# A reordered start, and model-axis results in frequency order with a new planner figure, in an attention-plus-Fourier kernel

## The chip, the cores and the metric

One Trainium2 chip, one core. The metric is device time of one execution in microseconds (us). TensorE is called PE below (its weight loads PEld), VectorE is DVE, ScalarE is ACT, GpSimd is POOL.

Words used below: to turn is to transpose on TensorE. TensorE is warm where it runs at full rate and cold where it runs at half rate, as with four score matmuls that take 0.92 us in one place and 1.65 us in another; the gate is the clock gate that the prediction cites. A line of a trace is start and duration in us, engine, line of the kernel, operation, output<-inputs and count; in brackets stands how long the engine was idle before and what ended that wait (the releaser). A ratio with two numbers behind it is given with its 95% interval.

## The reference, cut to what matters

```python
# q, k, v: (4 batches, 8 heads, 768, 64) fp32; sampled_blocks: (24, 3)
scores = scale * q @ k.T                         # per head
mask   = window | first/last block | sampled blocks   # 24 x 24 blocks of 32
attn   = softmax(where(mask, scores, -1e9)) @ v
x      = attn, heads side by side                # (4, 768, 512)
mixed  = real(fft(fft(x, axis=1), axis=2))       # sequence axis, then model axis
u      = x + mixed
un     = (u - mean(u)) / sqrt(var(u) + 1e-6)
out    = u + relu(un @ w_ch1) @ w_ch2            # 512 -> 2048 -> 512
```

## The kernel before

Attention runs in 96 slots of two units (a unit is one chunk of 128 keys for one half of the queries of a head pair). The Fourier and channel work of a batch is done between the attention slots of the next one. So the mixing of the first batch runs between the slots of the second; I call the last part of this, about 220 to 300 us, "the stage". The order in which an engine gets its instructions is fixed when the kernel is built: a small planner keeps a clock for each engine, and takes the next piece of mixing work when the durations it has been told say that it fits.

```python
def d(us, fn, *args):                      # a piece of VectorE work, told to last `us`
    return "d", lambda: fn(*args), 0.0, 0.0, us
...
ar = [[d(1.7 if m == 1 and half == 1 else 1.3, arrive, half, m) for m in range(T)]
      for half in range(2)]
...
def gap(rest=0.0, ahead=None, kinds="tm"):
    ...
    while apart:
        kind, fn, pe, act, dve, need = apart[0]
        ...
        if kind in "dw":
            ...
            if max(when["DVE"], state["ready"]) + dve > when["PE"] + rest + ahead:
                break
```

The start: k and q of the first head pair are turned on TensorE in the one bank of pool "t", and q's six copies go out on VectorE, behind both tables of the block mask.

```python
spread_q(off_q[0:NB, :], maskT)
twice(off_q)
spread_q(keep_q[0:NB, :], keep)            # second table, needed later
...
def turn(n, a, half):
    tp, at = ps_t.tile([P, 512], FP32, tag="t", name="tp"), bank("t")
    ...
    for c, part in enumerate(parts):
        nc.tensor.transpose(tp[:, c * P:(c + 1) * P], part, ident)
    ...
        copy = nc.vector.tensor_copy if n == 0 else nc.scalar.copy
        for to, to_jump, frm, jump, cnt, step in _TURNED[half]:
            copy(out=_grid(dst, to, 2, to_jump, cnt, 1),
                 in_=_grid(tp, frm, 2, jump, cnt, step))
```

The model axis: five products make the cosine and sine parts of one block of 128 rows, even frequencies first and odd ones after them. `arrive` then adds them to two row blocks of x, each with four additions of 127 or 128 columns and one of two.

```python
def across(m):
    across_p(ps, slice(0, P), ks)          # even cosine (two products), odd cosine
    ...
    nc.tensor.matmul(ps[:, KD:KD + QD - 1], zs[:, 0, ks], sd_sb[:, 0:QD - 1],
                     start=True, stop=True)
    nc.tensor.matmul(ps[:, KD + QD - 1:512], zs[:, 1, ks], sd_sb[:, QD - 1:KD - 2],
                     start=True, stop=True)
    ...
def arrive(half, m):
    ...
    for src, up, op in ((un[:, KD:512], half == 0, ALU.subtract),
                        (un[:, 2:KD], half == 1, ALU.add)):
        for odd in range(2):
            n = QD - 1 + odd
            at = src[:, 0:QD - 1] if odd == 0 else src[:, QD - 1:KD - 2]
            f = 1 if odd else 2
            xs = _run(x, f if up else DM - f, n, 2 if up else -2)
            tt(out=xs, in0=xs, in1=at, op=op)
```

From the second batch on GpSimd adds up the softmax terms, beside VectorE:

```python
if c == 1:
    nc.gpsimd.tensor_add(out=acc_of[n, half], in0=e_of[u - 1], in1=e)
elif c > 1:
    nc.gpsimd.tensor_add(out=acc_of[n, half], in0=acc_of[n, half], in1=e)
```

Of the kernel before, what the change touches and what calls it, by code (L numbers as in the profile page):

```python
# [11 lines left out]
FP32 = mybir.dt.float32  # L12
BF16 = mybir.dt.bfloat16
U8 = mybir.dt.uint8
I32 = mybir.dt.int32
# [72 lines left out]
def kernel(  # L88
# [165 lines left out]
    def bit(n):  # L254
# [8 lines left out]
    load_q(0)  # L263

    nc.scalar.activation(out=sm.tile([P, 1], FP32, tag="nm", name="nm"), in_=neg_half,
                         func=ACT.Exp)
    load_v(0, nc.scalar)

    nc.vector.memset(maskT, 0.0)
    for base, cm, pat, fill in (  # L270
# [17 lines left out]
    twice(of_k)  # L288
    kb_i = bit(1).bitcast(I32)
    nc.gpsimd.iota(kb_i, pattern=[[0, 1]], base=0, channel_multiplier=1)  # L290
    kb = bit(1)
# [16 lines left out]
    twice(off_q)  # L308
    spread_q(keep_q[0:NB, :], keep)

    def mask_step(i):
# [29 lines left out]
    def table_d(src, dst):  # L341
# [7 lines left out]
        def put():  # L349
            if dst is cd_sb:  # L350
                nc.vector.memset(alt, 0.0)
                for to, frm in ((dst, raw), *((alt[g:g + 1, :], row) for g in (0, 32, 64))):
                    nc.vector.tensor_copy(out=to[:, 0:1], in_=frm[:, KD - 1:KD])
                    nc.vector.tensor_copy(out=to[:, 1:QD + 1], in_=frm[:, 0:KD - 2:2])
                nc.vector.tensor_copy(out=dst[:, QD + 1:KD], in_=raw[:, 1:KD:2])
            else:
                nc.vector.tensor_copy(out=dst[:, 0:QD - 1], in_=raw[:, 2:KD - 2:2])
                nc.vector.tensor_copy(out=dst[:, QD - 1:KD - 2], in_=raw[:, 1:KD:2])
                nc.vector.tensor_copy(out=dst[0:1, QD - 1:KD - 2], in_=row[:, 1:KD:2])
# [68 lines left out]
    def turn(n, a, half):  # L428
# [4 lines left out]
        dst = turned[n, a]  # L433
        tp, at = ps_t.tile([P, 512], FP32, tag="t", name="tp"), bank("t")
        if a == 0:
# [6 lines left out]
        if a == 1:  # L442
            nc.scalar.copy(out=dst[:, half * HS:(half + 1) * HS], in_=tp[:, 0:HS])
            give(at, busy("ACT", 0.5, done))
        else:
            copy = nc.vector.tensor_copy if n == 0 else nc.scalar.copy
            for to, to_jump, frm, jump, cnt, step in _TURNED[half]:
                copy(out=_grid(dst, to, 2, to_jump, cnt, 1),
                     in_=_grid(tp, frm, 2, jump, cnt, step))
                end = busy("DVE" if n == 0 else "ACT", 0.27 if cnt > 1 else 0.18, done)  # L450
            give(at, end)
# [161 lines left out]
    def fourier(b, xA, xB, uns):  # L613
# [94 lines left out]
        def across_p(ps, rows, ks):  # L708
            zc, zl = st["zc"], st["zs"][0:96, 2, :]
            mm = nc.tensor.matmul  # L710
            mm(ps[rows, 0:QD + 1], zc[:, 0, ks], cd_sb[:, 0:QD + 1], start=True, stop=False)
            mm(ps[rows, 0:QD + 1], zl[:, ks], alt, start=False, stop=True)
            mm(ps[rows, QD + 1:KD], zc[:, 1, ks], cd_sb[:, QD + 1:KD], start=True, stop=True)

        def across(m):
# [5 lines left out]
            if m == 1:  # L721
# [3 lines left out]
                give(bank("t"), when["PE"] + 2.0)  # L725
            nc.tensor.matmul(ps[:, KD:KD + QD - 1], zs[:, 0, ks], sd_sb[:, 0:QD - 1],
                             start=True, stop=True)
            nc.tensor.matmul(ps[:, KD + QD - 1:512], zs[:, 1, ks], sd_sb[:, QD - 1:KD - 2],
                             start=True, stop=True)
# [3 lines left out]
            if m == 1:  # L733
                nc.scalar.copy(out=st["zs"][0:1, 0, 0:KD], in_=end[0:1, 0:KD])
            tt(out=un[:, KD:512], in0=ps[:, KD:512], in1=un[:, 2:KD], op=ALU.subtract)
            tt(out=un[:, 2:KD], in0=ps[:, KD:512], in1=un[:, 2:KD], op=ALU.add)  # L736

        def arrive(half, m):
# [3 lines left out]
            if m == 1 and half == 1:  # L742
                row = st["zs"][0:1, 0, :]
                nc.vector.tensor_copy(out=un[0:1, 0:KD], in_=row[:, 0:KD])
                nc.vector.tensor_scalar(out=un[0:1, KD:512], in0=row[:, 2:KD],
                                        scalar1=-1.0, scalar2=None, op0=ALU.mult)
            for src, up, op in ((un[:, KD:512], half == 0, ALU.subtract),
                                (un[:, 2:KD], half == 1, ALU.add)):
                for odd in range(2):
                    n = QD - 1 + odd  # L750
                    at = src[:, 0:QD - 1] if odd == 0 else src[:, QD - 1:KD - 2]
                    f = 1 if odd else 2
                    xs = _run(x, f if up else DM - f, n, 2 if up else -2)
                    tt(out=xs, in0=xs, in1=at, op=op)
            xs = _run(x, M, 2, -M)
            tt(out=xs, in0=un[:, 0:2], in1=xs, op=ALU.add)

# [24 lines left out]
        def d(us, fn, *args):  # L782
# [6 lines left out]
        pq = [("m", lambda m=m: across(m), 2.6 if m == 1 else 1.6, 0.7, 0.95) for m in range(T)]  # L789
        ar = [[d(1.7 if m == 1 and half == 1 else 1.3, arrive, half, m) for m in range(T)]  # L790
              for half in range(2)]
# [368 lines left out]
    turn(0, 1, 0)  # L1160
    turn(0, 0, 0)
    w_loads()
    for sl in range(B * SB + 1):
# [112 lines left out]
```

## Time and profile before

| | before |
|---|---|
| time, median (range), the first 3 of the 4 runs below | 1135.9 us (1134.07 to 1137.52) |
| profiled span | 1132.1 us |
| TensorE busy | 1079.4 us (95%) |
| first scores start | 11.10 us |
| the stage, 232.07 to 305.61 us | 73.54 us, of which TensorE busy 61.55 |

The prediction shows and reads the page, the table by windows and the two soft places. One thing it does not show is where the wait of 2.54 us before the last transposes comes from. This is VectorE of the kernel before just ahead of it:

```profile
287.71 1.39 DVE L779 TENSOR_SCALAR un<-x,st 128x512 f32<-128x512 f32 x1
...
291.75 0.55 DVE L779 TENSOR_SCALAR un<-x,st 128x512 f32<-128x512 f32 x1 [1.83 <-POOL st L769]
292.75 0.55 DVE L779 TENSOR_SCALAR un<-x,st 128x512 f32<-128x512 f32 x1 [0.46 <-POOL st L769]
```

VectorE itself is idle for 1.83 us there: the normalising row needs a reciprocal root that GpSimd makes between its sums. So the chain is TensorE for VectorE for GpSimd.

### The profile page before, as it was taken

To read this page: it belongs to the slowest core of one execution; us is meant where nothing else is said; L and a number is where in the kernel's file an instruction comes from. 1 tells how busy PE (TensorE), PEld (TensorE's weight loads), DVE (VectorE), ACT (ScalarE), POOL (GpSimd) and SP (SyncE) were. 2 spreads that over 40 slices of the span, in tenths; PEclk is the share of its full clock that TensorE was granted. 3 is DMA by queue.
4 is the path that set the end of the run, shared out by engine and by line. 5 is a ranking of instruction groups with operands and counts; after the bars stand their busy time and mean duration, and the time that the engine had idled before them with its cause. 6 is when DMAs were issued, how large, how long until landed. Compare 5 with 4: busy or idle time off the path is not lost.

```text
span 1132.1 us, 11978 instructions
## 1 busy us (share of the span) xinstructions
PE 1079.4 (95%) x4284; PEld 516.3 (46%) x4284; DVE 643.9 (57%) x1195; ACT 391.4 (35%) x809; POOL 250.1 (22%) x182
## 2 busy tenths in 40 slices
PE   6999988978899999999999999999999999999997
PEld 2333333433445545444444555454354555544553
DVE  4888888488764634554459455544456355533431
ACT  4888755545212012354443211244330202210110
POOL 1000067557300000244536100243440001000000
PEclk9999999989899999999999999999999999999999
DMA  6757321011000000201111000111000001000001
GB/s 196 209 165 221 95 53 46 15 43 43 1 0 1 1 0 10 65 24 43 34 23 28 1 0 1 50 48 29 1 1 0 1 1 29 28 1 0 1 0 59
DMA packets 65184, 44.27 MB, mean 39 GB/s; under 512 B 52814, under 2 KB 57948, under 8 KB 65116
## 3 DMA queue, kind: packets, MB, share of 16 engines
q1 hardware_dynamic: 63228, 42.62, 13.4%
q10 hardware_dynamic: 1856, 0.79, 0.3%
q8 instruction: 36, 0.59, 0.2%
q14 instruction: 32, 0.26, 0.1%
q0 software_dynamic: 32, 0.01, 0.0%
HBM read 37.11 MB, written 6.29 MB: 38 GB/s over the span
## 4 chain that ended last, share of the span: by engine, by line
PE 85%; DVE 8%; ACT 2%; issue 2%; DMA 1%; SPq 1%; POOL 1%; ACTq 0%; DVEq 0%; POOLq 0%
PE y L942 29%; PE z L889 15%; PE s L470 10%; PE o L512 8%; PE yp L889 7%; PE xp L889 4%; DVE e L491 3%; PE tp L440 2%; PE zp L701 1%; PE sp L559 1%; DMA wraw<-in_moe_w_ch_dram 1%; PE xt L530 1%; PE zp L672 1%; PE s L475 1%; PE sp L573 1%
## 5 line engine op out<-in xcount | busy, mean ns | idle before, releaser
L500 POOL TENSOR_TENSOR acc<-acc,e 128x768 f32<-128x768 f32 x96 | 179.3, 1868 | 110.5 <-DVE e L491 105.8
L470 PE MATMUL s<-qT,kT 64*128 64x384 f32 x768 | 164.3, 533 | 14.7 <-DVE e L491 11.5
L945 DVE TENSOR_TENSOR x<-y,x 128x512 f32<-128x512 f32 x96 | 66.3, 691 | 195.0 <-PE y L942 194.8
L491 DVE TENSOR_TENSOR e<-s,mask 128x768 f32<-128x768 f32 x144 | 131.2, 950 | 72.9 <-ACT s L489 70.2
L942 PE MATMUL y<-w_sb,hB 128*128 128x512 f32 x384 | 170.2, 594 | 1.1 <-DVE x L945 1.0
L942 PE MATMUL y<-w_sb,hA 128*128 128x512 f32 x384 | 170.6, 593 | 0.6 <-ACT zs L703 0.6
L512 PE MATMUL o<-e,vr 128*64 128x384 f32 x768 | 145.1, 499 | 0.0
L489 ACT ACTIVATE s<-s 128x768 f32<-128x768 f32 x144 | 109.6, 795 | 70.3 <-PE s L470 69.4
L942 PEld LDWEIGHTS y<-w_sb,hB 128*128 128x128 f32 x384 | 71.5, 190 | 86.8 <-issue 81.9
L942 PEld LDWEIGHTS y<-w_sb,hA 128*128 128x128 f32 x384 | 71.2, 190 | 82.5 <-issue 79.5
L894 DVE TENSOR_TENSOR hA<-z,hA 128x384 f32<-128x384 f32 x64 | 35.7, 558 | 119.8 <-PE z L889 119.8
L498 POOL TENSOR_TENSOR acc<-e 128x768 f32<-128x768 f32 x24 | 46.3, 1928 | 246.5 <-DVE e L491 184.0
L470 PEld LDWEIGHTS s<-qT,kT 64*128 64x128 f32 x768 | 63.4, 189 | 75.8 <-DVE e L491 30.4
L889 PE MATMUL z<-unT,t 128*128 128x384 f32 x256 | 93.0, 486 | 0.0
L767 POOL TENSOR_SCALAR st<-st 128x1 f32<-128x1 f32 x24 | 6.6, 274 | 347.7 <-DVE st L766 347.3
L512 PEld LDWEIGHTS o<-e,vr 128*64 128x64 f32 x768 | 46.6, 136 | 75.6 <-issue 74.0
L898 ACT ACTIVATE hA<-hA 128x384 f32<-128x384 f32 x64 | 33.4, 522 | 119.4 <-DVE hA L894 118.9
L889 PEld LDWEIGHTS z<-unT,t 128*128 128x128 f32 x256 | 48.6, 190 | 33.9
L898 ACT ACTIVATE hB<-hB 128x384 f32<-128x384 f32 x64 | 33.5, 523 | 85.4 <-DVE hB L894 85.4
L909 ACT COPY hA<-xp 128x384 f32<-128x384 f32 x32 | 15.3, 478 | 134.4 <-PE xp L889 134.4
L889 PE MATMUL xp<-unT,w_sb 128*128 128x384 f32 x128 | 48.5, 502 | 1.5 <-ACT zs L703 1.1
L889 PE MATMUL yp<-unT,w_sb 128*128 128x384 f32 x128 | 47.4, 493 | 0.2 <-DVE un L736 0.2
(172 smaller groups left out, 1239.6 us busy)
## 6 DMA issues: line engine op xcount, KB each, us to landing
wraw<-in_moe_w_ch_dram SPq DMA_DIRECT2D x32, 512.0 KB
qr<-in_q_dram SPq DMA_DIRECT2D x90, 64.0 KB
vr<-in_v_dram SPq DMA_DIRECT2D x30, 192.0 KB
kr<-in_k_dram SPq DMA_DIRECT2D x28, 192.0 KB
out_dram<-x SPq DMA_DIRECT2D x16, 128.0 KB
out_dram<-x SPq DMA_DIRECT2D x8, 256.0 KB
out_dram<-x SPq DMA_DIRECT2D x8, 126.0 KB
out_dram<-x SPq DMA_DIRECT2D x4, 252.0 KB
```

The costliest lines, as they stand in the source:

```text
L440: nc.tensor.transpose(tp[:, c * P:(c + 1) * P], part, ident)
L470: nc.tensor.matmul(s[:, i, 0:HS], kT[D * i:D * i + D, c * P:(c + 1) * P], qT[D * i:D * i + D, half * HS:(half + 1) * HS], start=True, stop ...
L489: nc.scalar.activation(out=s[:, :, 0:HS], in_=s[:, :, 0:HS], func=ACT.Exp, scale=scale)
L491: nc.vector.tensor_tensor(out=e, in0=s[:, :, 0:HS], in1=m.broadcast_to([P, 2, HS]), op=ALU.mult)
L498: nc.gpsimd.tensor_add(out=acc_of[n, half], in0=e_of[u - 1], in1=e)
L500: nc.gpsimd.tensor_add(out=acc_of[n, half], in0=acc_of[n, half], in1=e)
L512: nc.tensor.matmul(o[D * i:D * i + D, :], vt[:, i, c, :], e[:, i, :], start=(c == 0), stop=(c == C - 1))
L889: nc.tensor.matmul(to, a[:, k, :], c[:, k, :], start=(k == 0), stop=(k == ND // 2 - 1))
L894: tt(out=to, in0=ps, in1=a, op=ALU.add)
L898: nc.scalar.activation(out=h, in_=h, func=ACT.Relu)
L942: nc.tensor.matmul(y, hs[half][:, l, m * P:(m + 1) * P], w2_sb[:, 4 * r + l, :], start=(l == 0), stop=(l == 3))
L945: nc.vector.tensor_tensor(out=x[:, m, :], in0=y, in1=x[:, m, :], op=ALU.add)
```

## The change

Intent at the start: have the first scores begin earlier and at full rate. Idle products keep TensorE at work before and after the first turns; q's first turn uses its own bank; its copies alternate between VectorE and ScalarE; the second mask table goes behind them. Intent on the model axis: the products write their results to PSUM with a stride of two, so that frequencies lie in order, and `arrive` needs one addition per part of 255 columns in place of two. The planner is told 1.0 us for an `arrive` in place of 1.3.

```diff
+    def warm(n):
+        m = ps_m.tile([P, P], FP32, tag="m", name="warm")
+        for _ in range(n):
+            nc.tensor.matmul(m, ident, ident, start=True, stop=True)
+    warm(6)
 ...
+    kb_i = bit(1).bitcast(I32)          # moved up, ahead of six selects
+    nc.gpsimd.iota(kb_i, pattern=[[0, 1]], base=0, channel_multiplier=1)
 ...
-    spread_q(keep_q[0:NB, :], keep)     # moved behind the first turns
 ...
-        tp, at = ps_t.tile([P, 512], FP32, tag="t", name="tp"), bank("t")
+        first = n == 0 and half == 0
+        tag, pool = ("m", ps_m) if first and a == 0 else ("t", ps_t)
+        tp, at = pool.tile([P, 512], FP32, tag=tag, name="tp"), bank(tag)
 ...
+                on, copy = (("DVE", nc.vector.tensor_copy) if n == 0 and (half == 1 or i % 2 == 0)
+                            else ("ACT", nc.scalar.copy))
 ...   # across_p likewise for the cosine products
-            nc.tensor.matmul(ps[:, KD:KD + QD - 1], zs[:, 0, ks], sd_sb[:, 0:QD - 1],
+            nc.tensor.matmul(_run(ps, KD + 1, QD - 1, 2), zs[:, 0, ks], sd_sb[:, 0:QD - 1],
                              start=True, stop=True)
-            nc.tensor.matmul(ps[:, KD + QD - 1:512], zs[:, 1, ks], sd_sb[:, QD - 1:KD - 2],
+            nc.tensor.matmul(_run(ps, KD, QD, 2), zs[:, 1, ks], sd_sb[:, QD - 1:KD - 2],
                              start=True, stop=True)
 ...   # arrive: two halves of each part become one
+                xs = _run(x, 1 if up else DM - 1, M - 1, 1 if up else -1)
+                tt(out=xs, in0=xs, in1=src, op=op)
 ...
-        ar = [[d(1.7 if m == 1 and half == 1 else 1.3, arrive, half, m) for m in range(T)]
+        ar = [[d(1.4 if m == 1 and half == 1 else 1.0, arrive, half, m) for m in range(T)]
 ...
     turn(0, 0, 0)
+    warm(3)
+    spread_q(keep_q[0:NB, :], keep)
     w_loads()
```

Cut: the merged copies of the cosine table, and the shifted slices that follow from the new order of the frequencies.

More of the change, by code (lines that the diff above doesn't have):

```diff
@@ L288 @@
     twice(of_k)
-    kb_i = bit(1).bitcast(I32)
-    nc.gpsimd.iota(kb_i, pattern=[[0, 1]], base=0, channel_multiplier=1)
     kb = bit(1)
@@ L352, in put @@
                 for to, frm in ((dst, raw), *((alt[g:g + 1, :], row) for g in (0, 32, 64))):
-                    nc.vector.tensor_copy(out=to[:, 0:1], in_=frm[:, KD - 1:KD])
-                    nc.vector.tensor_copy(out=to[:, 1:QD + 1], in_=frm[:, 0:KD - 2:2])
+                    nc.vector.tensor_copy(out=to[:, 0:QD + 1], in_=frm[:, 0:KD:2])
                 nc.vector.tensor_copy(out=dst[:, QD + 1:KD], in_=raw[:, 1:KD:2])
@@ L445, in turn @@
         else:
-            copy = nc.vector.tensor_copy if n == 0 else nc.scalar.copy
-            for to, to_jump, frm, jump, cnt, step in _TURNED[half]:
+            for i, (to, to_jump, frm, jump, cnt, step) in enumerate(_TURNED[half]):
+                on, copy = (("DVE", nc.vector.tensor_copy) if n == 0 and (half == 1 or i % 2 == 0)
+                            else ("ACT", nc.scalar.copy))
                 copy(out=_grid(dst, to, 2, to_jump, cnt, 1),
                      in_=_grid(tp, frm, 2, jump, cnt, step))
-                end = busy("DVE" if n == 0 else "ACT", 0.27 if cnt > 1 else 0.18, done)
+                end = busy(on, 0.27 if cnt > 1 else 0.18, done)
             give(at, end)
@@ L709, in across_p @@
             zc, zl = st["zc"], st["zs"][0:96, 2, :]
+            even, odd = _run(ps[rows, :], 0, QD + 1, 2), _run(ps[rows, :], 1, QD, 2)
             mm = nc.tensor.matmul
-            mm(ps[rows, 0:QD + 1], zc[:, 0, ks], cd_sb[:, 0:QD + 1], start=True, stop=False)
-            mm(ps[rows, 0:QD + 1], zl[:, ks], alt, start=False, stop=True)
-            mm(ps[rows, QD + 1:KD], zc[:, 1, ks], cd_sb[:, QD + 1:KD], start=True, stop=True)
+            mm(even, zc[:, 0, ks], cd_sb[:, 0:QD + 1], start=True, stop=False)
+            mm(even, zl[:, ks], alt, start=False, stop=True)
+            mm(odd, zc[:, 1, ks], cd_sb[:, QD + 1:KD], start=True, stop=True)
         def across(m):
@@ L734, in across @@
                 nc.scalar.copy(out=st["zs"][0:1, 0, 0:KD], in_=end[0:1, 0:KD])
-            tt(out=un[:, KD:512], in0=ps[:, KD:512], in1=un[:, 2:KD], op=ALU.subtract)
-            tt(out=un[:, 2:KD], in0=ps[:, KD:512], in1=un[:, 2:KD], op=ALU.add)
+            tt(out=un[:, KD:512], in0=ps[:, KD:512], in1=un[:, 1:M], op=ALU.subtract)
+            tt(out=un[:, 1:M], in0=ps[:, KD:512], in1=un[:, 1:M], op=ALU.add)
         def arrive(half, m):
@@ L744, in arrive @@
                 nc.vector.tensor_copy(out=un[0:1, 0:KD], in_=row[:, 0:KD])
-                nc.vector.tensor_scalar(out=un[0:1, KD:512], in0=row[:, 2:KD],
+                nc.vector.tensor_scalar(out=un[0:1, KD:512], in0=row[:, 1:M],
                                         scalar1=-1.0, scalar2=None, op0=ALU.mult)
             for src, up, op in ((un[:, KD:512], half == 0, ALU.subtract),
-                                (un[:, 2:KD], half == 1, ALU.add)):
-                for odd in range(2):
-                    n = QD - 1 + odd
-                    at = src[:, 0:QD - 1] if odd == 0 else src[:, QD - 1:KD - 2]
-                    f = 1 if odd else 2
-                    xs = _run(x, f if up else DM - f, n, 2 if up else -2)
-                    tt(out=xs, in0=xs, in1=at, op=op)
-            xs = _run(x, M, 2, -M)
-            tt(out=xs, in0=un[:, 0:2], in1=xs, op=ALU.add)
+                                (un[:, 1:M], half == 1, ALU.add)):
+                xs = _run(x, 1 if up else DM - 1, M - 1, 1 if up else -1)
+                tt(out=xs, in0=xs, in1=src, op=op)
+            ends = x[:, 0:M + 1:M]
+            tt(out=ends, in0=un[:, 0:M + 1:M], in1=ends, op=ALU.add)
         norms = {}
```

## The prediction

> **What bounds the kernel now.** I read the page first (busy shares and the chain that ended last), then a table of stages by window, then the timeline of each stage that TensorE does not fill, and last the forms of the lines that the change touches.
>
> ```profile
> PE 1079.4 (95%) x4284; PEld 516.3 (46%) x4284; DVE 643.9 (57%) x1195; ACT 391.4 (35%) x809; POOL 250.1 (22%) x182
> ...
> PE 85%; DVE 8%; ACT 2%; issue 2%; DMA 1%; SPq 1%; POOL 1%; ACTq 0%; DVEq 0%; POOLq 0%
> ```
>
> TensorE (PE) is busy for 1079.4 of 1132.1 us and is 85% of the chain. A change that takes no TensorE work away can earn only from the 53 us of idle time, or from stretches where TensorE runs at a lower granted clock. The stages show where both lie (columns: window, PE, PEld, DVE, ACT, POOL busy us with counts, granted clock, DMA share, GB/s):
>
> ```profile
> 0.00:10.00 10.00, 1.99 (x7) 1.22 (x7) 6.61 (x37) 1.96 (x3) 3.68 (x14) 1.00 0.74 188
> 10.00:20.00 10.00, 8.90 (x44) 3.00 (x44) 1.27 (x9) 4.32 (x7) 0.00 (x0) 1.00 0.81 236
> ...
> 265.00:300.00 35.00, 28.27 (x138) 13.48 (x137) 29.04 (x44) 15.60 (x33) 21.81 (x18) 0.90 0.14 35
> 300.00:500.00 200.00, 198.82 (x659) 103.35 (x658) 108.37 (x219) 45.83 (x97) 20.70 (x21) 1.00 0.05 14
> 500.00:750.00 250.00, 248.08 (x959) 121.77 (x958) 138.09 (x235) 82.06 (x178) 75.29 (x49) 1.00 0.10 26
> ```
>
> From 300 us on TensorE is over 99% busy at full clock: there nothing on VectorE (DVE) or ScalarE (ACT) sets the end. The two soft places are the first 20 us and the end of the second attention batch (about 220 to 295 us), where DVE is busy 29.04 of 35 us and the granted clock is 0.90.
>
> The start, in order of time (start, us, engine, instruction, idle before and its releaser):
>
> ```profile
> 5.12 0.14 DVE L292 CAST scratch<-scratch 24x1 f32<-24x1 int32 x1 [0.71 <-POOL scratch L290]
> ...
> 5.44 0.87 PE L440 MATMUL tp<-ident,kr 128*128 128x128 f32 x3 [5.44 <-DMA kr<-in_k_dram]
> ...
> 6.88 1.12 PE L440 MATMUL tp<-ident,qr 128*128 128x128 f32 x4 [0.57 <-ACT kT L443]
> ...
> 9.12 1.13 DVE L245 CAST at_q<-wide 24x128 bf16<-24x128 f32 x10
> 10.18 1.12 DVE L448 COPY qT<-tp 128x128 f32<-128x128 f32 x6
> 11.10 1.65 PE L470 MATMUL s<-qT,kT 64*128 64x384 f32 x4 [3.10 <-DVE qT L448]
> ...
> 15.51 0.92 PE L470 MATMUL s<-qT,kT 64*128 64x384 f32 x4
> ```
>
> q's turn waits 0.57 us for kT's copy, because both turns use the one bank of pool "t". The first scores wait 3.10 us for qT: VectorE is spreading the second table of the block mask until 10.25, and only then makes all six qT copies. The same four score matmuls take 1.65 us there and 0.92 us at 15.51: until about 15 us the array runs at half rate.
>
> The soft stage around 220 to 295 us, first VectorE with GpSimd (POOL) beside it, in three views (wide, GpSimd's own, narrow), then TensorE:
>
> ```profile
> 222.26 3.54 DVE L754 TENSOR_TENSOR x<-x,un 128x127 f32<-128x127 f32 x4
> ```
> ```profile
> 221.63 3.83 POOL L500 TENSOR_TENSOR acc<-acc,e 128x768 f32<-128x768 f32 x2 [2.71 <-DVE e L491]
> ```
> ```profile
> 222.26 1.32 DVE L754 TENSOR_TENSOR x<-x,un 128x127 f32<-128x127 f32 x1
> ...
> 223.71 1.90 DVE L754 TENSOR_TENSOR x<-x,un 128x127 f32<-128x127 f32 x1
> ...
> 225.53 0.28 DVE L754 TENSOR_TENSOR x<-x,un 128x128 f32<-128x128 f32 x1
> ```
> ```profile
> 289.16 0.66 PE L816 MATMUL utp<-ident,un 128*128 128x128 f32 x4 [1.63 <-DVE un L779]
> 292.35 2.18 PE L816 MATMUL utp<-ident,un 128*128 128x128 f32 x8 [2.54 <-DVE un L779]
> 294.32 2.77 PE L889 MATMUL xp<-unT,w_sb 128*128 128x384 f32 x4
> ...
> 305.61 1.45 PE L889 MATMUL xp<-unT,w_sb 128*128 128x384 f32 x4
> ```
>
> The four additions of one part of the model-axis result take 3.54 us, though three other rows of the kind are 0.28 us each: the first ends when GpSimd's first sum ends, the second when its second does, the rest run free. At the stage's end TensorE has only transposes left, waits 1.63 and 2.54 us for VectorE's normalised rows, and then does the first product in 2.77 us instead of 1.45: cold again.
>
> **What the Trainium skill says.** (1) "TensorE: Matmul & The Clock Gate", Part 1: the array starts at half rate and goes to full rate after about 3.4 us of sustained work, in a free-running window. The 1.65 against 0.92 us agrees, about 4 us after the first scores. (2) The same page, Part 4: transposes don't count as busy for that gate. This fits the turns at 5.44 and 6.88 not having warmed it, and is why the added idle products are plain ident-by-ident matmuls. (3) "SBUF — State Buffer", Who interferes with whom: a VectorE instruction with two SBUF inputs and a GpSimd one that reads SBUF block each other for whole instructions. The 1.32 and 1.90 us above agree. (4) "PSUM — Partial Sum Buffer", Specifications: lines of 8 bytes, and "any non-contiguous AP slows matmuls significantly". No matmul of the kernel before writes with a stride, so its trace says nothing; after the change all five matmuls of every model-axis result do.
>
> **The change part by part.**
>
> Start. The small iota goes ahead of six GpSimd selects, so VectorE loses its 0.71 us wait: the mask chain moves from 5.12 to about 4.45, and ends its first table at 7.86 instead of 8.53. q's turn uses a bank of "m", so it follows kr's turn at 6.3 and ends near 7.4. Of the six copies three (128, 126, 126 columns) stay on VectorE, 0.6 us as half of the 1.12 plus the larger shapes; three go to ScalarE, which has only kT's copy (6.35 to 6.83). The second table's spread (8.54 to 10.18, 1.64 us) goes behind the copies; its product is first needed by the mask steps of the fourth slot, near 37 us, so it costs nothing. qT is ready at 7.86 + 0.6 = 8.5 instead of 11.1: 2.6 us earlier.
> Six idle products start when ident is ready (2.53), each two instructions of 0.22 us warm, so about 0.43 cold: 2.6 us, ended near 5.2, before kr lands at 5.44. Three more fill 7.4 to 8.7, beside the copies. Two cold units of scores took 11.10 to about 15.0, 3.9 us; two warm ones from 15.51 take 2.2. If the gate opens in time that is another 1.7 us; because its window is free-running I count 1.2. Sum: 3.8 us (2.6 to 4.3). It lasts: from 40 to 110 us TensorE is 98% busy, so nothing slack swallows it.
>
> Model axis, work. Each part's four additions (median 285 ns, 1.14 us) become two of 255 columns, 0.42 us each as the rows of that size (L735) show: 0.3 us less, 24 parts, 7 us of VectorE. After 300 us this is hidden (18 of 24 parts). In the soft stage six parts count: 6 x 0.3 = 1.8 us at most, and less where GpSimd blocks, since two additions still meet two sums. The table copies lose four small instructions: nothing on the path.
>
> Model axis, order. The planner is told 1.0 us for a part, not 1.3. Comparing the instruction orders, TensorE's order is the same in both kernels but for the start and this stage: the second model-axis product comes two slots earlier, and the six transposes of normalised rows, four of them bunched at the end before, are spread so that one is left. That takes away most of 1.63 + 2.54 us and some of the cold product after it (1.3 us). Against it, VectorE was busy 56.3 of the 67.6 us from 226.7 to 294.3, so part of the wait only moves earlier: I count 4 us saved in all, the 1.8 included (0 to 8).
>
> Model axis, TensorE. If the stride is free, 0. If it doubles the five products, 12 results x 5 x 0.22 = 13 us, plus 4 edge sets x 3 x 0.22 = 2.6 us: some 15 us, nearly all exposed.
>
> Sum without the stride: 1135.9 - 3.8 - 4.0 = 1128.1.
>
> **The rivals.** Strided PSUM writes: the skill speaks for them. Against: in the chain of waits an fp32 score product of 384 columns takes 0.42 us and a bf16 one 0.135, so at fp32 there may be time to spare between two writes. I give a clear slowdown a chance of 0.25; then 1135.9 - 7.8 + 15 = 1143.
> A wait in place of the one removed: the stage at 220 to 295 stays bound by VectorE locked against GpSimd, now with TensorE stopped in mid-slot for the earlier transposes and products; the gain is 0 to 1 and the time 1131 to 1132. For it: 11.5 us of scores already wait on the mask multiply:
>
> ```profile
> PE s L470 <- DVE e L491: 11.5, 11, 1.9
> ```
> Data that lands too late for an earlier start: q of the second pair is issued until 11.7 us and its turn moves from 19.96 to about 16; weight chunk 1 would be wanted near 20. I think both have landed; if not, 1 to 2 us of the 3.8 are lost.
>
> **Range and chances.** Most likely 1128, pulled up by the stride to 1129. A range for 8 in 10 is 1120 to 1142: the low end is 4.3 at the start and all 8 and a little from the stage with its cold stretches; the high end is the stride at nearly full cost. 2% is 22.7 us: faster than 1113 would need more than all idle of the two places, slower than 1158 more than the doubled stride.
>
> **What would show it.** Right: the first scores near 8.5 us and their four matmuls near 0.92; additions of 255 columns, 24 x 2, near 0.42 us where GpSimd is idle; one transpose group left before the first product, and the granted clock of the stage above 0.93; rows after 300 us unchanged. The model-axis products decide the stride, by this row's successor (275 means free, above 400 means slow):
>
> ```profile
> L728 PE MATMUL pq<-sd_sb,zs x24: 274/276/422, 218.0 to 925.6; 128*128 128x128 f32 x24
> ```
> I am wrong if the first scores are still cold or wait for DMA, if the stage is as long as before, or if those rows grow.

## The result, and the profile after

| | before | after |
|---|---|---|
| time, median (range), 4 runs each | 1134.99 us (1132.92 to 1137.52) | 1122.39 us (1120.79 to 1124.91) |
| ratio, 95% interval | | 0.989 (0.9859 to 0.9921) |
| profiled span, granted clock | 1132.1, 0.990 | 1122.8, 0.993 |
| first scores | 11.10 us | 9.18 us |
| the stage | 73.54 us | 64.55 us |

A ratio here and below is the mean time of one kernel's runs over that of the kernel before in the same rounds, so it is not quite the ratio of the medians. The changed kernel is 1.1% faster: within 2%, and 6.6 us below the 1129 on record.

The page of the changed kernel, and its windows (length, busy us of PE, PEld, DVE, ACT, POOL with counts, granted clock, DMA share, GB/s):

```profile
PE 1081.5 (96%) x4302; PEld 518.5 (46%) x4302; DVE 636.3 (57%) x1140; ACT 392.4 (35%) x812; POOL 250.4 (22%) x182
...
PE 86%; DVE 8%; ACT 2%; issue 2%; POOL 1%; DMA 0%; SPq 0%; ACTq 0%; DVEq 0%; POOLq 0%
```
```profile
0.00:10.00 10.00, 6.94 (x29) 5.74 (x29) 6.63 (x32) 2.56 (x6) 3.69 (x14) 1.00 0.75 192
10.00:20.00 10.00, 9.60 (x47) 3.27 (x43) 1.07 (x10) 4.92 (x10) 0.00 (x0) 1.00 0.82 238
265.00:300.00 35.00, 30.28 (x143) 15.45 (x139) 27.72 (x41) 14.91 (x32) 20.79 (x16) 1.00 0.05 12
300.00:500.00 200.00, 198.82 (x660) 103.17 (x660) 104.88 (x202) 46.39 (x99) 23.71 (x22) 1.00 0.05 14
```

TensorE's busy time has not fallen but grown by 2.1 us: the idle products at the start add 4.4 us (2.93 and 1.49). From 300 to 500 us the row is the same as before, 198.82 us busy of 200, and from the end of the stage to the end of the span it is 826.5 us before and 826.3 after. So the gain lies before that point, and the 7.6 us less of VectorE work over the whole kernel counted only where it fell.

The windows must be cut at the same work, not at the same time. From the scores of the 44th slot to the second channel product of the first batch, before and then after:

```profile
232.07:305.61 73.54, 61.55 (x301) 29.96 (x301) 59.41 (x91) 32.09 (x67) 41.74 (x32) 0.91 0.10 24
```
```profile
231.91:296.46 64.55, 55.87 (x290) 26.17 (x286) 54.96 (x78) 32.13 (x67) 41.21 (x30) 0.97 0.12 31
```

The changed kernel enters the stage at almost the same time and leaves it 9.0 us earlier. The idle time of TensorE (length less busy time) fell from 11.99 to 8.68 us; the rest is in the busy time, where the granted clock rose from 0.91 to 0.97. The counts differ because the order does, and some products fall outside the cut. A cut a little wider, 226.80 to 305.61 before and 226.66 to 296.46 after, holds 320 matmuls in both: there 4.8 us of the gain is idle time and 4.2 us is the same products at a higher clock.

The longest single wait of the old stage stands in its middle, and the prediction does not name it (TensorE, then the two VectorE lines ahead of it, all of the kernel before):

```profile
245.43 0.66 PE L440 MATMUL tp<-ident,qr 128*128 128x128 f32 x4 [3.57 <-DVE sums L543]
...
247.83 2.82 PE L470 MATMUL s<-qT,kT 64*128 64x384 f32 x8
```
```profile
242.35 2.49 DVE L754 TENSOR_TENSOR x<-x,un 128x127 f32<-128x127 f32 x4
...
244.83 0.55 DVE L543 TENSOR_TENSOR sums<-sp,sums 128x384 f32<-128x384 f32 x1
```

A turn of q waits 3.57 us because the addition into `sums` stands in VectorE's queue behind a normalised row and four model-axis additions, and the scores after it run cold (2.82 us for eight matmuls that take 1.56 warm). This wait is 3.4 to 3.6 us in each kernel with the old order and all of GpSimd's sums, and it is in none with the new order. So the order takes away 3.57 us here and 3.7 at the end (below), and a new wait of 3.13 us comes.

The stage's end in the changed kernel, the place of the 1.63 and 2.54 us:

```profile
283.23 0.63 PE L821 MATMUL utp<-ident,un 128*128 128x128 f32 x4 [0.47 <-DVE un L784]
283.70 1.46 PE L894 MATMUL xp<-unT,w_sb 128*128 128x384 f32 x4
284.99 1.45 PE L894 MATMUL yp<-unT,w_sb 128*128 128x384 f32 x4
289.57 1.56 PE L894 MATMUL z<-t,w_sb 128*128 128x384 f32 x4 [3.13 <-DVE t L858]
```

One transposed row block is left, the wait is 0.47 us, and the first product runs at 1.46 us, warm. A new wait stands behind it: 3.13 us for VectorE, whose next additions are held up:

```profile
283.00 2.30 DVE L858 TENSOR_TENSOR t<-unT 128x512 f32<-128x512 f32 x1
285.34 2.18 DVE L858 TENSOR_TENSOR t<-unT,t 128x512 f32<-128x512 f32 x1
287.44 0.68 DVE L858 TENSOR_TENSOR unT<-unT 128x512 f32<-128x512 f32 x1
```

The same addition takes 0.68 us as soon as GpSimd's sums (three of them without a pause until 286.97) are over.

The start of the changed kernel, in order of time:

```profile
2.58 2.93 PE L269 MATMUL warm<-ident 128*128 128x128 f32 x12 [2.58 <-POOL ident masks.py:199]
...
7.27 0.66 PE L447 MATMUL tp<-ident,qr 128*128 128x128 f32 x2 [0.47 <-DMA qr<-in_q_dram]
...
8.02 0.29 DVE L456 COPY qT<-tp 128x128 f32<-128x128 f32 x1
8.34 0.27 ACT L456 COPY qT<-tp 128x128 f32<-128x128 f32 x1 [1.45 <-DVE qT L456]
8.64 0.29 DVE L456 COPY qT<-tp 128x126 f32<-128x126 f32 x1 [0.33 <-ACT qT L456]
8.96 0.16 ACT L456 COPY qT<-tp 128x2 f32<-128x2 f32 x1 [0.35 <-DVE qT L456]
9.16 0.29 DVE L456 COPY qT<-tp 128x126 f32<-128x126 f32 x1 [0.23 <-ACT qT L456]
...
9.18 1.65 PE L478 MATMUL s<-qT,kT 64*128 64x384 f32 x4
```

The copies on two engines do not run side by side: each starts when the one on the other engine is over, and names it as its releaser. The first scores begin after the fourth copy, while the last two still run (to 9.64 us). And the first scores take 1.65 us, half rate, in spite of the idle products.

The products' row by form (ns: lowest, median, highest) answers the question of the stride:

```profile
L737 PE MATMUL pq<-sd_sb,zs x24: 274/275/276, 218.0 to 916.3; 128*128 128x128 f32 x24
```

275 ns as before: writing fp32 results to PSUM with a stride of two costs nothing here. The medians of the other four products of a result, which now write with a stride too, are 274 and 275 ns, before and after.

### The profile page after: what moved, and what is told of

Its sections match the earlier page's. It is cut to its first block, busy times and chain, and to the rows that moved or that the text cites. A ratio compares the mean times of both kernels' runs of the same rounds, so it can differ in the third digit from the quotient of the medians.

```text
span 1122.8 us, 11958 instructions
## 1 busy us (share of the span) xinstructions
PE 1081.5 (96%) x4302; PEld 518.5 (46%) x4302; DVE 636.3 (57%) x1140; ACT 392.4 (35%) x812; POOL 250.4 (22%) x182
## 4 chain that ended last, share of the span: by engine, by line
PE 86%; DVE 8%; ACT 2%; issue 2%; POOL 1%; DMA 0%; SPq 0%; ACTq 0%; DVEq 0%; POOLq 0%
PE y L947 30%; PE z L894 15%; PE s L478 10%; PE o L520 9%; PE yp L894 7%; PE xp L894 4%; DVE e L499 3%; PE tp L447 2%; PE zp L709 1%; PE sp L567 1%; PE xt L538 1%; PE zp L680 1%; PE s L483 1%; DVE x L759 1%; PE sp L581 1%
## 5 line engine op out<-in xcount | busy, mean ns | idle before, releaser
L894 PE MATMUL z<-t,w_sb 128*128 128x384 f32 x128 | 46.6, 487 | 3.1 <-DVE t L858 3.1
```

The source lines that it names most:

```text
L894: nc.tensor.matmul(to, a[:, k, :], c[:, k, :], start=(k == 0), stop=(k == ND // 2 - 1))
```

## The experiments

Twelve runs in three groups; each group ran on one chip and shares its 11 runs of the kernel before (medians 1134.85, 1134.67 and 1135.09 us). The experiments have 4 to 6 runs each. Where a difference is given in us below, it is the ratio's distance from 1 times 1135. Executions of one kernel lie up to 7.4 us apart (1131.43 to 1138.84 for the kernel before in the first group), so the medians alone can't place differences under 2 us; for those I read the trace.

### 1. Which part pays: four parts alone

**The planner's figures alone.** The kernel before, with nothing but the assumed duration changed. TensorE's order in the stage is then that of the changed kernel.

```diff
-        ar = [[d(1.7 if m == 1 and half == 1 else 1.3, arrive, half, m) for m in range(T)]
+        ar = [[d(1.4 if m == 1 and half == 1 else 1.0, arrive, half, m) for m in range(T)]
```

> The kernel before with one edit: the planner is told 1.0 us for a part of the model-axis result instead of 1.3, so TensorE's order is exactly that of the changed kernel, while each part is still four strided additions and the start is the old one. Theory (the order is what pays): 6 to 9 us faster than the kernel before, the stage of 220 to 295 us shorter by as much, and only one group of transposes left before the first product. Rival (the additions pay, the order only follows): 0 to 2 us faster, or slower, because TensorE now waits in mid-slot for parts that still take 3.5 us.

Measured: 1127.77 us, ratio 0.9939 (0.9916 to 0.9962), 6.9 us less. Its stage:

```profile
234.03:299.11 65.08, 55.88 (x290) 26.14 (x286) 55.56 (x86) 32.28 (x68) 41.10 (x30) 0.97 0.12 31
```

65.08 us against 73.54: one number in the planner, with not one instruction less, gives 8.5 of the 9.0 us of the stage. The end of the stage is that of the changed kernel too:

```profile
285.88 0.63 PE L816 MATMUL utp<-ident,un 128*128 128x128 f32 x4 [0.50 <-DVE un L779]
286.34 1.46 PE L889 MATMUL xp<-unT,w_sb 128*128 128x384 f32 x4
```

**The additions alone.** Frequency order and one addition per part, with the planner still told 1.3; TensorE's order is that of the kernel before.

```diff
 # the changed kernel's across_p, across, arrive, table copies; old start; and
-        ar = [[d(1.4 if m == 1 and half == 1 else 1.0, arrive, half, m) for m in range(T)]
+        ar = [[d(1.7 if m == 1 and half == 1 else 1.3, arrive, half, m) for m in range(T)]
```

> The changed kernel's results in frequency order with one addition per part, but the planner told 1.3 us as before, so TensorE's order is exactly that of the kernel before, and with the old start. Theory (order pays): 0.5 to 2 us faster than the kernel before, six parts on the path at 0.3 us at most. Rival (work pays): 5 to 9 us faster. Strided results in PSUM: if they cost anything on TensorE, this run is slower than before; the trace of the changed kernel says they do not.

Measured: 1134.95 us, ratio 0.9993 (0.9966 to 1.0019): no difference to be seen. Stage 72.25 us, and the waits at its end stand:

```profile
290.31 0.66 PE L812 MATMUL utp<-ident,un 128*128 128x128 f32 x4 [1.63 <-DVE un L775]
293.51 2.18 PE L812 MATMUL utp<-ident,un 128*128 128x128 f32 x8 [2.54 <-DVE un L775]
295.48 2.11 PE L885 MATMUL xp<-unT,w_sb 128*128 128x384 f32 x4
```

Halving the number of additions saves 1.3 us of the stage in the old order. The VectorE time of these additions from 205 to 300 us shows why: 19.03 us before, 18.20 with fewer of them, but 13.74 with only the new order and 12.93 with both. What a part costs is decided by what GpSimd does beside it. Two additions of 255 columns, in the changed kernel, once with GpSimd idle and once with it at work:

```profile
219.69 0.75 DVE L759 TENSOR_TENSOR x<-x,un 128x255 f32<-128x255 f32 x2
...
222.26 3.41 DVE L759 TENSOR_TENSOR x<-x,un 128x255 f32<-128x255 f32 x2
```

Four small additions took 3.54 us at that place. Two additions against two GpSimd sums are still two waits for a whole sum.

**The whole model axis, old start.**

```diff
 # the changed kernel without: warm, the iota's move, keep_q's move,
 # q's bank of "m", copies on two engines
```

> The whole model-axis part of the change with its planner figures, and the old start. Theory: 9 to 10 us faster than the kernel before, which is the whole gain that the two profiled traces show from 220 us on. If the start carries a large share instead, this is only 5 to 7 us faster.

Measured: 1126.91 us, ratio 0.9924 (0.9901 to 0.9946), 8.6 us less, just under the 9 to 10 expected; stage 64.54 us, as in the changed kernel.

**The whole start, old model axis.**

```diff
 # the kernel before with: warm(6), warm(3), the iota's move, keep_q's move,
 # q's bank of "m", copies on two engines
```

> The whole start of the changed kernel (nine idle products, earlier iota, q turned in another bank, copies on two engines, second mask table later) and nothing of the model axis. Theory from the two traces: 1 to 3.5 us faster than the kernel before, with the first four scores still at 1.65 us where the idle products have not opened the clock gate in time, and 0.92 where they have. My prediction had 3.8 us and 0.92 us.

Measured: 1129.76 us, ratio 0.9951 (0.9932 to 0.9971), 5.6 us less, where 1 to 3.5 had been expected; stage 74.44 us, as before. The two halves add up to 14.2 us; the changed kernel is 12.5 us faster by its first ratio and 14.5 by a later one (below), so they are additive as far as the runs can tell. In this trace the first scores are at full rate:

```profile
9.16 0.92 PE L479 MATMUL s<-qT,kT 64*128 64x384 f32 x4 [1.08 <-ACT qT L457]
```

### 2. The start: idle products, the kind of turn, the copies

**No idle products.**

```diff
-    warm(6)
-    warm(3)
```

> The changed kernel without its nine idle products; everything else of the start stays. The start alone was 5.6 us faster than before. Theory A (the earlier copies and the clock share the gain): the scores still begin near 9.2 us, but at 1.65 us, and the array stays at half rate until somewhere between 13 and 24 us, as in the runs without idle products so far; the time is 2 to 4 us above the changed kernel, near 1125. Rival (the idle products never pay, because the transposes between them keep the gate shut): within 1 us of the changed kernel.

Measured: 1123.15 us, ratio 0.9909 (0.9887 to 0.9932). The first scores start as early (copies and mask order are untouched) but at half rate, until about 13 us:

```profile
9.15 1.65 PE L470 MATMUL s<-qT,kT 64*128 64x384 f32 x4 [2.30 <-ACT qT L448]
...
13.47 0.92 PE L470 MATMUL s<-qT,kT 64*128 64x384 f32 x4
```

This is 10.3 us less than before, against 12.5 and 14.5 for the changed kernel, so by the ratios the idle products are worth 2.2 to 4.2 us, with an uncertainty of about 4 (by the medians 0.8 to 2.4); two variants with idle products on the same chip, below, have medians of 1119.75 and 1119.99. The new model axis alone gave 8.6, which leaves only 1.7 us, with an uncertainty of about 4, for the earlier copies. The one profile speaks the other way (the mark described below, 23.3 us here, against 27.2 with the old start and 22.4 with all of the new). Which of the two is the larger part of the start stays open.

**First turns as ordinary products** in place of transposes, in case transposes do not help to open the clock gate.

```diff
-            nc.tensor.transpose(tp[:, c * P:(c + 1) * P], part, ident)
+            if first:
+                nc.tensor.matmul(tp[:, c * P:(c + 1) * P], part, ident, start=True, stop=True)
+            else:
+                nc.tensor.transpose(tp[:, c * P:(c + 1) * P], part, ident)
```

> The changed kernel with the first two turns done as ordinary products with ident, not as transposes, so that TensorE does ordinary products from 2.6 us to the first scores. Theory (transposes do not count for the gate): the first scores are at 0.92 us in every profile, the spread of the times is smaller, and the time is 0 to 2 us below the changed kernel, though the turns take about 1 us longer at half rate. Rival (transposes count as well as products): no difference in when the gate opens, and 0 to 1 us slower.

Measured: 1119.75 us, ratio 0.9878 (0.9855 to 0.99). First scores warm:

```profile
9.17 0.92 PE L481 MATMUL s<-qT,kT 64*128 64x384 f32 x4 [0.72 <-ACT qT L459]
```

**All six q copies on ScalarE.**

```diff
-                on, copy = (("DVE", nc.vector.tensor_copy) if n == 0 and (half == 1 or i % 2 == 0)
+                on, copy = (("DVE", nc.vector.tensor_copy) if n == 0 and half == 1
```

> The changed kernel with all six copies of q's first turn on ScalarE, none on VectorE. In the changed kernel the copies of the two engines alternate and none overlaps: each waits for the one before on the other engine. Theory (two engines take turns at one bank, so splitting buys nothing, and VectorE starts late because of the mask): copies from 7.9 us without a break, first scores near 8.7 instead of 9.2, time 0.3 to 0.7 us below the changed kernel, so within its noise. Rival (splitting does help): first scores later than 9.2 us.

Measured: 1119.99 us, ratio 0.9869 (0.9847 to 0.9891).

```profile
7.92 1.03 ACT L456 COPY qT<-tp 128x128 f32<-128x128 f32 x6 [1.25 <-PE tp L447]
...
9.09 1.65 PE L478 MATMUL s<-qT,kT 64*128 64x384 f32 x4
```

One engine takes 1.03 us for all six and the scores start at 9.09, no later than with two engines, which need 1.62 us for the six (8.02 to 9.64). The 8.7 expected was missed: in this profile TensorE comes to the scores straight from its three idle products, which at half rate last from 7.67 us until about then, though the last copy ended at 8.95. So the second engine brings nothing by itself; by the traces, what brings the scores forward is that the copies no longer stand behind the second mask table, which VectorE spread until 10.25 us in the kernel before. No run moved the table alone.

**Both of these together.**

```diff
 # the two edits above in one kernel
```

> The changed kernel with two more edits of the start together: the first two turns as ordinary products, and all six copies of q's first turn on ScalarE. Expected: first scores near 9.0 us at 0.92 us in the profile, 2 to 3 us below the changed kernel run again beside it, near 1119 to 1120, with a smaller spread. Rival: the same within 1 us, if the gate opens before the scores in most runs of the changed kernel anyway.

Measured: 1120.55 us, ratio 0.9863 (0.9841 to 0.9885). The first scores are warm but start at 9.38 us, not near 9.0, and the time is within about 1 us of the changed kernel: the rival held.

**The changed kernel once more**, in the same group as this.

```diff
 # no edit
```

> The changed kernel once more, beside the others on one chip: 1121 to 1124 us, a spread of some 4 us between runs, the slow ones those in which the first scores are at half rate.

Measured: 1120.75 us, ratio 0.9872 (0.985 to 0.9894), a little below the expected range, with a spread of 2.3 us. The three variants of the start lie within 1 us of it, with overlapping intervals: none beats it.

```profile
9.16 0.92 PE L478 MATMUL s<-qT,kT 64*128 64x384 f32 x4 [1.05 <-ACT qT L456]
```

This run of the very same program has its first scores at full rate, where its earlier profile had them at half. Over all profiles with idle products the first scores were warm in 6 of 8, without them in 0 of 6. With ordinary-product turns it was 2 of 2, with transposes 4 of 6: too few to say that the kind of turn matters. The two cold profiles are of the slowest executions of their kernels: 1124.91 us (the others 1120.79 to 1123.89) and 1123.74 (1118.99 to 1120.26). The first of them also holds a second cold spell, told of below.

How much the gate is worth shows best in the experiment with the old start and the new model axis. Its window from 20 to 25 us, and after it the same window of the kernel before:

```profile
20.00:25.00 5.00, 4.90 (x22) 1.43 (x20) 0.00 (x0) 0.88 (x2) 0.00 (x0) 1.00 0.53 207
```
```profile
20.00:25.00 5.00, 3.88 (x26) 1.71 (x24) 1.23 (x5) 3.79 (x12) 0.00 (x0) 1.00 0.69 257
```

TensorE is busy 98% of the time and does 22 matmuls; in the other it does 26 in 3.88 us and then has to wait. Note that the column of the granted clock says 1.00 in both: at the start that column does not show the half rate, only the durations do. I took the time of the third slot's exponentials as a mark. With the old start it was 25.3 us in the profile of before, but 26.2, 26.4, 28.5 and 29.6 in the four others: the gate opened at about 15 us in the one that I predicted from and up to 24 us in the others. With the whole new start and its idle products it was 21.6 to 24.5, 22.4 in the mean of eight profiles. The mean of the five old starts is 27.2.

### 3. The stage: why the order pays

**The kernel before without most of GpSimd's sums.** Wrong (relative error 1.656: the softmax sums lack terms); it shows what VectorE and TensorE do when GpSimd is out of the way.

```diff
-        elif c > 1:
-            nc.gpsimd.tensor_add(out=acc_of[n, half], in0=acc_of[n, half], in1=e)
```

> The kernel before without GpSimd's sums from the third unit on (wrong results on purpose, as in the run on the changed kernel, which fell from 1122 to 1103 us). Theory (the stage is long because VectorE is blocked by GpSimd, and the new order pays by letting TensorE work meanwhile): without the sums the order hardly matters, so this comes to 1106 to 1110 us, the changed kernel's 1103 plus the start's 4 to 6, and the four additions take 1.1 us. Rival (the old order wastes time by itself, with VectorE free as well): 1112 us or more.

Measured: 1114.69 us, ratio 0.9813 (0.9786 to 0.984).

**The changed kernel with the same edit**, wrong in the same way.

```diff
-        elif c > 1:
-            nc.gpsimd.tensor_add(out=acc_of[n, half], in0=acc_of[n, half], in1=e)
```

> The changed kernel without GpSimd's sums from the third unit on (wrong results on purpose: the softmax sums lack four of six terms). TensorE's order is unchanged. Theory (the stage from 220 to 295 us is bound by VectorE blocked by GpSimd's sums): the two additions of a part fall from 2.3 to 3.4 us to about 0.75 everywhere, the waits of TensorE in the stage fall from about 10 us to under 4, and the time falls by 5 to 12 us, since the batches' first folds before 200 us are blocked as well. Rival (VectorE's own work bounds the stage): 0 to 3 us faster.

Measured: 1102.95 us, ratio 0.9727 (0.9701 to 0.9752). The stages, first in the kernel before, then in the changed one, both without these sums:

```profile
226.26:289.73 63.47, 58.27 (x301) 28.50 (x301) 45.06 (x90) 32.31 (x68) 12.64 (x16) 0.95 0.13 34
```
```profile
218.94:275.30 56.36, 53.50 (x289) 25.86 (x286) 45.11 (x78) 31.58 (x67) 11.75 (x14) 1.00 0.14 36
```

Two things follow. GpSimd's sums cost the stage 73.54 - 63.47 = 10.1 us in the old order and 64.55 - 56.36 = 8.2 in the new, and 18 to 20 us of the whole kernel (1135.1 to 1114.7, 1120.8 or 1122.4 to 1103.0): that is what the sums cost here, VectorE's waiting for them and any waiting for the sums themselves taken together, and more than the 5 to 12 us expected of the changed kernel. And the new model axis (the order, with its fewer additions) still saves 63.47 - 56.36 = 7.1 us of the stage with the sums gone. My theory was that the new order pays because TensorE now has work while VectorE is locked out by GpSimd; then the old order without the sums should have fallen to 1106 to 1110 us. It stood at 1114.69, and the rival (the old order is bad in itself) had said 1112 or more. By the trace the theory falls. By the times it is less sharp: the two ratios differ by 9.8 us with an uncertainty of about 4, and 5.6 (about 2) of that is the start, which leaves 4 with an uncertainty of about 5. So how much of the order's worth needs GpSimd stays open.

What is bad in the old order shows without the sums as well:

```profile
275.73 0.66 PE L814 MATMUL utp<-ident,un 128*128 128x128 f32 x4 [0.59 <-DVE un L777]
277.03 0.66 PE L814 MATMUL utp<-ident,un 128*128 128x128 f32 x4 [0.64 <-DVE un L777]
278.43 1.09 PE L814 MATMUL utp<-ident,un 128*128 128x128 f32 x4 [0.75 <-ACT unT L815]
279.31 2.52 PE L887 MATMUL xp<-unT,w_sb 128*128 128x384 f32 x4
```

Row block after row block is normalised and turned at the end, with nothing else left for TensorE; from 275.73 to 279.31 us it works about two thirds of the time (0.66 + 0.66 + 1.09 of 3.58), its rate falls, and the product after them takes 2.52 us instead of 1.45. In the new order they are spread among the slots. This is a part of the gain that the table showed as clock, and not all of it. My estimate from the durations of the kernel before, against the same products at full rate in the same trace: three cold spells, 1.7 us at 232 to 237, 1.5 at 247 to 251 behind the wait for `sums`, and 2.9 at the end; the changed kernel has one, 1.6 us at 257 to 261. Whether the waits or the transposes, or both, let the rate fall is not separated by any run.

**A still smaller figure for the planner**, 0.7, in the changed kernel.

```diff
-        ar = [[d(1.4 if m == 1 and half == 1 else 1.0, arrive, half, m) for m in range(T)]
+        ar = [[d(1.1 if m == 1 and half == 1 else 0.7, arrive, half, m) for m in range(T)]
```

> The changed kernel with the planner told 0.7 us for a part (1.1 for the one with the edge row) instead of 1.0: parts are put earlier still, and some transposes of normalised rows, q and k change places. If the gain is only a matter of telling the planner a small figure, this is 0 to 3 us faster than the changed kernel; if 1.0 happens to be a good order, or VectorE blocked by GpSimd sets the pace by now, it is the same within 2 us or slower.

Measured: 1124.47 us, ratio 0.9902 (0.9882 to 0.9922), about 3 us slower than the changed kernel in the same rounds. Its stage:

```profile
227.70:296.02 68.32, 56.09 (x291) 26.22 (x291) 55.51 (x76) 32.19 (x67) 40.82 (x30) 0.98 0.12 30
```

The clock is as high as in the changed kernel, but idle time is 12.23 us in place of 8.68: work placed too early makes TensorE wait in mid-slot (1.9 us of it before an edge product, for `sums`). So it is not that smaller is better. The figure is a choice between bunching at the end and waiting in the middle, and it needs no truth: the real duration of a part here is 0.75 or 3.4 us, and neither is 1.0.

## Why the prediction was right or wrong

The class (within 2%) and the range (1120 to 1142) held, and 1122.39 lies near the low end. The sum was 3.8 + 4.0 = 7.8 us; measured were 5.6 and 8.6. Both terms came out too small, in part for reasons that the prediction did not have, and the range that took in the result was wide because of a stride that cost nothing: so far the hit is luck.

- **The order of the model axis: mechanism right, the term mis-sized.** The prediction put it, with the 1.8 us of work, at 4 (0 to 8), because "part of the wait only moves earlier". The runs show 8.6 us in all, 6.9 by the order alone. The waits of 1.63 and 2.54 us did fall to 0.47. Two things were not counted: the wait of 3.57 us for `sums` in the middle of the stage, and the clock, 4.2 us over the whole stage, of which the prediction had only 1.3 us of one cold product. A part of the wait did move, as said: the 3.13 us before the first z product.
- **The work of the model axis: right to be small, and smaller still.** At most 1.8 us were allowed in the stage. The trace gives 1.3 in the old order and about 0.5 in the new (65.08 against 64.54), the times 0.8 with an interval around zero.
- **The stride: right at the value given the larger chance.** 275 ns after, 276 before. The chance of 0.25 given to the slow case is what pulled 1128.1 up to 1129.
- **The start: the first step failed, and the sum still came out too small.** "qT is ready at 7.86 + 0.6 = 8.5" took for granted that copies on two engines run side by side. They wait for each other: the first four, which the first scores need, take 1.10 us from 8.02 on, where 0.6 us was counted for all six, and all six take 1.62 us, longer than the 1.03 us on ScalarE alone. The Trainium skill, "PSUM — Partial Sum Buffer", section "PSUM bank collisions raise a hardware error", says that two engines must not access one bank in the same quadrant at once, reads among them, and that the compiler's scheduler puts a dependency between such instructions. All six copies read the one tile `tp`, one bank; the trace agrees with that reading by its alternation at 8.02, 8.34, 8.64, 8.96 us. No run here used two banks, and all six also write the one tile `qT`, which could order them as well; so the cause is argued and only the alternation is shown. The scores came at 9.16 to 9.18, a gain of 1.9 and not 2.6.
- **The gate: the term that was too small.** The prediction took 3.9 us for two cold units, from a profile in which the gate opened at about 15 us, and counted 1.2. In the other old starts it opened later. The mark at the third slot moves by 27.2 - 22.4 = 4.8 us in the mean; 1.9 is the earlier start and 2.9 is the gate (with whatever else sits between). Cold first scores were also a sign of being wrong that the prediction named; the first profile showed it, and 6 of the 8 profiles did not.
- **The rival of the lock between VectorE and GpSimd** was real as a cost (8 to 10 us of the stage) but did not eat the gain: from 205 to 300 us TensorE's scores waited 4.7 us for the mask multiply before and 4.4 us after.
- **Late data: did not come where it was looked for.** The last two transposes of q's first turn do wait 0.47 us for their transfer, but VectorE, which makes the first copy, is busy with the mask until 7.98 us, later than they end (7.93). From 9 to 40 us TensorE of the changed kernel waits for no transfer at all, so the second head pair and the weights had landed.
- **What one profile can hide:** in the profiled run of the changed kernel the start's gain is gone by 232 us. Here it lost it, in an attention slot of the second batch; then the same work in the later run of the same kernel, behind the turn of the same q:

```profile
150.76 2.21 PE L478 MATMUL s<-qT,kT 64*128 64x384 f32 x8
152.90 2.50 PE L520 MATMUL o<-e,vr 128*64 128x384 f32 x8
```
```profile
148.11 1.56 PE L478 MATMUL s<-qT,kT 64*128 64x384 f32 x8
149.60 1.51 PE L520 MATMUL o<-e,vr 128*64 128x384 f32 x8
```

2.50 against 1.51 us for the same eight products: a spell near half rate. Of the 9.3 us between the two first profiles 9.0 therefore come from the stage, while the timed runs have the start's share on average.

## What to carry to other kernels

Where a build-time planner decides the order, try its assumed durations by themselves before removing work: here one such number was worth more than halving the instructions that it describes, and a still smaller one was worse. Read a stage's gain as idle time and as clock apart, since a bunch of small waits and transposes came with slow products behind it (2.77 us instead of 1.45). And count on two engines sharing a copy only when you have seen the two overlap in a trace.

## What the Trainium skill lacked or had wrong

- "PSUM — Partial Sum Buffer", Specifications, says of its 8-byte lines that "any non-contiguous AP slows matmuls significantly". For fp32 products of 128 columns written with a stride of two it did not: 274 to 276 ns, 275 in the median, against 274 contiguous at best and 276 in the median before.
- "TensorE: Matmul & The Clock Gate", Part 1, gives about 3.4 us of sustained work until full rate, in a free-running window. It adds that the number of slow products varies from run to run and that the gate has been seen stuck. Here the wait was longer than that: scores from 11.1 us on ran at half rate until about 15 us in one profile and until about 24 us in another, with TensorE 99% busy from 11 to 25 us in the latter (13.82 of 14 us); and in 2 of 8 profiles even idle products and turns from 2.58 us on left the scores at 9.1 us cold.
- The same page, Part 4, says that transposes do not count as busy for the gate. The transposes at the stage's end before (the product after them 2.77 us instead of 1.45) are in keeping with it, but the waits between them stand as a second cause; turns made as ordinary products (2 of 2 profiles warm against 4 of 6) do not settle it.
- "SBUF — State Buffer", Who interferes with whom, agrees with the traces. What this case adds is the size: two additions of 0.75 us in all became 3.41, and the kernel lost 18 to 20 us to GpSimd's sums.
